# Whole-row attention units of a block-sparse attention + MLP kernel, spread over two chunks

## The chip, the cores and the metric

The kernel runs on one core of a Trainium2 chip. The metric is the device time of one execution in microseconds (us). Each core has TensorE (PE, with a separate row PEld for its weight loads), VectorE (DVE), ScalarE (ACT), GpSimd (POOL) and SyncE (SP, which here only issues transfers). Each engine takes its instructions in the order in which they were written for it and waits at semaphores for the others.

## The reference, cut to what matters

```python
batch, n_heads, seq, head_dim = (4, 8, 768, 64);  block = 32
scores = scale * q @ k.T                       # per batch and head
mask   = |blk_i - blk_j| <= 1  or  first/last block of queries or keys  or  3 sampled blocks per query block
attn   = softmax(where(mask, scores, -1e9));   a = attn @ v
x      = a as [3072 tokens, 512]
out    = relu(x @ w_in) ** 2 @ w_out           # d_ff = 2048
```

A query block in the middle of the sequence sees 8 key blocks. The first and the last query block of a batch (64 rows per head) see all 768 keys: these are the whole rows.

## The kernel before, in words

**Tiling.** The 3072 tokens are 24 tiles of 128, three tiles to a chunk, so 8 chunks, two to a batch. For a chunk the MLP runs over 16 slices `f` of d_ff: `hidden` (L894) makes 12 matmuls into a PSUM tile `ph`, ACT makes `r` (relu) and `gh` (its square, rounded), DVE `gf` (the square in full), POOL `gl = gf - gh`; two slices later `project` (L920) multiplies `gh` and `gl` with `wo` into three accumulators `po`. In that time `wi` and `wo` of a coming slice are split: a DVE cast (L847) for the high part and a POOL subtraction (L848) for the low part.

**Attention beside it.** While PE works on the MLP of chunk c, the attention of chunk c+1 is laid between its matmuls. There are two kinds of unit. A `Half` is one tile's sparse rows for four heads: scores `s` (PE), maxima `m` and difference `p` (DVE), 16 exps that also move 32x32 blocks to other partitions, `pm` (ACT, L481), a transpose `pT` (DVE, L487), values `pv` (PE), normalisation (DVE). A `Whole` is a batch's whole rows for one pair of heads, four to a batch (`pr` 0 to 3): scores `g` (PE, L624), maxima (DVE), two exps `pg` (ACT, L649), 16 copies of 32x192 blocks `pgm` that alternate between POOL and ACT (L660), a transpose `pTg` (DVE, L666), values `pvg` (PE, L694), normalisation (DVE).

**What sets the order.** The order is written out: the MLP is a generator, and each of its yields is one step, about 96 to a chunk and 6 to a slice `f`. A unit is a generator too; what it yields is the number of steps until its next part is issued. `LAG` holds these numbers. A half starts every 16 steps (`STEP`), six to a chunk. For a whole the parts stand at: scores 0, exps 4, copies from 8 (two in a step, so eight steps), transpose at 20, values at 39. What a step holds for an engine is put in that engine's queue at that place, and nothing passes it later.

**Where the wholes stood.** `units(c)` gave a batch's four wholes to its first chunk, 16 steps apart, each 6 steps (`G_AT`) behind a half. So all four wholes of batch 1 stand beside the MLP of chunk 0 (its end) and 1, those of batch 2 beside chunk 2 (its end) and 3, those of batch 3 beside chunk 4 (its end) and 5. Chunks 2 and 4 carry six halves and only the beginning of the next wholes.

**Buffers.** `pT` and `pTg` share two buffers. A half's `pT` is used 11 steps after its transpose (`v`), a whole's `pTg` 19 steps after (`w`). Split weights `wi`, `wo` and `pg`, `pgm` share seven buffers (tag `w`). There is one buffer for each half of the keys of a batch (`kn`), one for its values (`vn`, in two halves one after the other), and one for its whole-row queries (`QG`).

**Loads.** SP issues nearly all transfers in one queue. Keys of the next batch were asked for in the fifth tile of a batch (`NT - 2`), the whole-row queries and values in the sixth.

```python
LAG = {"s": 0, "e": 4, "v": 11, "x": 4, "t": 4, "c": 0, "v0": 13, "w0": 4, "w": 19, "n": -1}
```

Of the kernel before, what the change touches and what calls it, by code (L numbers as in the profile page):

```python
# [22 lines left out]
B, H, S, D = 4, 8, 768, 64  # L23
# [4 lines left out]
NT = S // P  # L28
NJ = P // BLK
NPAIR = H // 2  # L30
# [32 lines left out]
STEP = PIECES // (2 * UC)  # L63
EARLY = 23
LAST = 4
LAG = {"s": 0, "e": 4, "v": 11, "x": 4, "t": 4, "c": 0, "v0": 13, "w0": 4, "w": 19, "n": -1}

G_AT = 6

STEP_0 = 5  # L70
STEP_1, FIRST_1 = 12, 0
LAG_1 = {**LAG, "v": 10, "x": 3, "t": 6, "v0": 5, "n": 0}
LAG_0 = {"s": 2, "x": 2, "t": 3, "c": 2, "v0": 2, "n": 2, "r": 1, "l": 3, "l0": 8}
# [23 lines left out]
def tile_block_sparse_attention_moe(ctx: ExitStack, tc, kd, knd, qd, qgd, vd, vnd, samp, const, wcat, out):  # L97
# [9 lines left out]
    nc = tc.nc  # L107
# [63 lines left out]
    def load_whole(b, eng=nc.sync):  # L171

        eng.dma_start(QG.rearrange("p a b -> p (a b)"), qgd[b])

    def load_keys(b, u, eng=nc.sync):

        kn = rot.tile([P, NBLK, 2, BLK], F32, tag=f"kn{u}", name=f"kn{b}_{u}", bufs=1)
        eng.dma_start(kn.rearrange("p a b c -> p (a b c)"), knd[b, u])
        st["kn", b, u] = kn
# [18 lines left out]
    def load_static(k, u, eng=nc.sync):  # L198
        us = halves(k, u)
        if us is None:  # L200
            return
        n = 1 if k == 0 else NJ
        for i in range(us.start, us.stop):
            src = columns(vd[order[k][0], V_STATIC * BLK :], i)
            src = src.unsqueeze(1).broadcast_to([2 * BLK, n, HW // 2])
            eng.dma_start(values_of(k)[0][0 : 2 * BLK, i, 0:n], src)
# [29 lines left out]
    def load_vn(b, hf, eng=nc.sync, own=None):  # L236

        vn = (own or rot).tile([P, NT, HW // 2], F32, tag="vn", name=f"vn{b}_{hf}", bufs=1)
        eng.dma_start(vn.rearrange("p t c -> p (t c)"), vnd[b, hf])
        st["vn", b, hf] = vn  # L240
# [19 lines left out]
    def load_q(b, t, eng=nc.sync, own=None):  # L260
        q = (own or rot).tile([P, NJ, NPAIR, BLK], F32, tag="q", name=f"q{b}_{t}", bufs=1 if own else 2)
        n = NJ * NPAIR * BLK
        eng.dma_start(q.rearrange("p a b c -> p (a b c)"), qd[b, :, t * n : (t + 1) * n])
        st["q", b, t] = q

    def keys_of(b, t, own=None):

        k = order.index((b, t))
        st["kg", b, t] = own.tile([P, NJ, NK, NPAIR, BLK], F32, name=f"KG{k}") if own else KG[(k - (k >= UC)) % 2]
# [5 lines left out]
    def copy_keys(b, t):  # L275

        vals = sampled(t, 0, POOL)
        k, kg = order.index((b, t)), st["kg", b, t]
        for u in range(2):
            copy = nc.gpsimd.tensor_copy  # L280
            if t < UC:
                static_keys(b, t, u, copy)
            if 0 < k < UC:
                key_edges(k, u, copy)
            else:
                key_windows(k, u, copy)
            kn = st["kn", b, u]
            for j in groups(t):
                for r in range(NRAND):
                    copy(  # L290
                        kg[:, j, key_place(k, j, r), 2 * u : 2 * u + 2].unsqueeze(1),
                        kn[:, bass.ds(vals[NRAND * j + r], 1)],
                    )
                yield
# [24 lines left out]
    def load_kg(b, t):  # L319
        vals = sampled(t, 0, SP)  # L320
        keys_of(b, t)
        k, kg, js = order.index((b, t)), st["kg", b, t], groups(t)
        k4 = kd[b].rearrange("p (a c) -> p a c", a=NBLK)
        for j in js:
            for r in range(NRAND):
                nc.sync.dma_start(
                    kg[:, j, key_place(k, j, r)].rearrange("p b c -> p (b c)").unsqueeze(1),
                    k4[:, bass.ds(vals[NRAND * j + r], 1), :],
                )
        src = k4[:, NJ * t + js[0] - 1]  # L330
        src = bass.AP(src.tensor, src.offset, [[NBLK * P, P], [P, len(js)], [1, 3 * P]])
        nc.sync.dma_start(kg[:, js[0] : js[-1] + 1, NK - 3 :].rearrange("p j a b c -> p j (a b c)"), src)
# [7 lines left out]
    def load_window(k, u, eng=nc.sync):  # L340
        us = halves(k, u)
        if us is None:
            return
        b, t = order[k]
        VB = values_of(k)[1]
        js = sorted(groups(t))
        j, c, n = js[0], NJ * t + js[0], len(js)
        for i in range(us.start, us.stop):
            src = vd[b, (c - 1) * BLK : (c + 1 + n) * BLK, i * HW // 2 : (i + 1) * HW // 2]
            src = bass.AP(src.tensor, src.offset, [[HW, 3 * BLK], [BLK * HW, n], [1, HW // 2]])  # L350
            eng.dma_start(VB[BLK:P, i, j : j + n], src)

    def load_sampled(k, u, eng, on, which=range(NRAND)):
        us = halves(k, u)
        if us is None:
            return
        b, t = order[k]
        VA, VB = values_of(k)
        vals = sampled(t, 1, on)
        v4 = columns(vd[b], us).rearrange("(a p) u c -> p a u c", p=BLK)  # L360
        for j in sorted(groups(t)):
            for r in which:
                a = (place(k, j, 3) if r == 2 else 2 + r) * BLK
                dst = (VB if r == 2 else VA)[a : a + BLK, us, j]
                eng.dma_start(dst.unsqueeze(1), v4[:, bass.ds(vals[NRAND * j + r], 1)])
# [14 lines left out]
    class Half:  # L380
# [172 lines left out]
        def loads(self, step):  # L553

            k = order.index((self.b, self.t))
            eng = nc.gpsimd if self.b == 0 else nc.sync
            if step == 0 and self.t == NT - 2 and self.b + 1 < B:
                load_keys(self.b + 1, self.u, eng)
            if step == 0 and self.t == NT - 1 and self.b + 1 < B:
                if self.u == 0:  # L560
                    load_whole(self.b + 1, eng)
                    load_vn(self.b + 1, 0, eng)
            n = k + (UC if k < UC - 1 else UC - 1)
            if step == 0 and self.u == 1 and k != UC - 1 and n < len(order):
                load_q(*order[n])
                if n < 2 * UC:
                    keys_of(*order[n])
                    later.append(copy_keys(*order[n]))
                    next(later[-1])
                elif self.moved:  # L570
                    load_kg(*order[n])
            if step == 1 and self.u == 1 and 2 * UC <= n < len(order):
                load_kg(*order[n])
            n = UC if k == 0 else k + 1
            if step == 2 and k not in range(1, UC) and n < len(order):
                if self.t == NT - 1:
                    load_static(n, self.u)
                load_window(n, self.u)
                load_sampled(n, self.u, nc.sync, SP)

    class Whole:
# [71 lines left out]
        def move(self):  # L653

            self.pm = rot.tile([P, NJ, NT, BLK], F32, tag="w", name=f"pgm{self.name}", bufs=WBUFS)
            x = self.p.rearrange("p (k a s) -> p k a s", k=NT, a=NJ)
            for g in range(NJ):
                for a in range(NJ):
                    copy = nc.scalar.copy if a % 2 else nc.gpsimd.tensor_copy
                    copy(self.pm[a * BLK : (a + 1) * BLK, g], x[g * BLK : (g + 1) * BLK, :, a])  # L660
                    if a % 2:
                        yield 0

        def turn_blocks(self):
# [53 lines left out]
    def begins(c):  # L718

        return PIECES * c - min(c, 1) * LEAD * UC  # L720

    def units(c):

        halves = [Half(b, t, u) for b, t in order[c * UC : (c + 1) * UC] for u in range(2)]
        wholes = [] if c % 2 else [Whole(c // 2, pr) for pr in range(NPAIR)]
        if c == 0:
            return [(i * STEP_0, u) for i, u in enumerate(wholes + halves)]
        if c == 1:
            return [(i * STEP_1 + FIRST_1, u) for i, u in enumerate(halves)]
        at = begins(c - 1) - EARLY  # L730
        both = [(at + i * STEP, u) for i, u in enumerate(halves)]
        both += [(at + i * STEP + G_AT, u) for i, u in enumerate(wholes)]
        return sorted(both, key=lambda x: x[0])

    class Stream:
# [285 lines left out]
    first = copy_keys(0, 1)  # L1021
# [20 lines left out]
    for at, u in units(0):  # L1042
        work.add(at, 0, lambda u=u: u.run(side, LAG_0))
# [21 lines left out]
    for c in range(1, NCH):  # L1065
        for at, u in units(c):
            work.add(at, c, lambda u=u, lag=LAG_1 if c == 1 else LAG: u.run(bank, lag))
    now = 0
# [71 lines left out]
```

## Time and profile before

| what | value |
|---|---|
| time, median of 3 runs | 744.15 us (743.92 to 744.68) |
| the profiled execution, its own time | 745.86 us |
| its span, first to last instruction | 744.0 us |
| PE busy | 714.0 us, 96% of the span |
| PE weight loads busy | 569.7 us, 77% |
| DVE busy | 533.0 us, 72% |
| ACT busy | 500.5 us, 67% |
| POOL busy | 539.4 us, 73% |
| mean granted TensorE clock | 0.991 |

The profile is of one execution. A row of a group reads: line, engine, operation, output <- input, shapes, count, busy time and mean duration of one, then the idle time of the engine just before such instructions and who ended it. A row of the timeline reads: start, duration, engine, line, operation, count, and in brackets the idle time before it with the instruction that ended it. A row of waits reads: who waited for whom, total us, times, longest. Below, "stretch c" is the time from the first `ph` matmul of chunk c to that of chunk c+1; in it the MLP of chunk c and the attention of chunk c+1 run.

### The profile page before, as it was taken

How to read it: one execution, taken by the hardware profiler on the slowest of the kernel's cores; microseconds unless marked ns; L12 is line 12 of the kernel's file. 1: busy time of each engine (PE TensorE's matmuls, PEld its weight loads, DVE VectorE, ACT ScalarE, POOL GpSimd, SP SyncE). 2: the span in 40 equal slices, each digit the busy share in tenths (PEclk: the TensorE clock that was granted, in tenths of full speed). 3: DMA queues.
4: the chain of work that ended last, by engine and by line, in shares of the span. 5: the costliest groups of instructions: out<-in, count | busy, mean ns of one | idle time of the engine just before them, and what ended most of it. 6: DMA issues, size and time to landing. Idle time of an engine off the chain costs nothing.

```text
span 744.0 us, 21519 instructions
## 1 busy us (share of the span) xinstructions
PE 714.0 (96%) x7496; PEld 569.7 (77%) x7496; DVE 533.0 (72%) x1076; ACT 500.5 (67%) x1107; POOL 539.4 (73%) x681
## 2 busy tenths in 40 slices
PE   5869999999999999999999999999999999999997
PEld 2546666567878888877878888877778888888996
DVE  7885766968776877768877786768778686647552
ACT  5875677998875875579776777478866776623222
POOL 7986734249786587769877577877976586868985
PEclk9988999999999999999999999999999999999999
DMA  8785799755555547645455466455355452101001
GB/s 271 226 225 159 206 298 304 179 154 171 146 126 130 174 126 211 145 104 144 104 165 146 100 193 177 132 131 176 95 160 143 100 160 55 34 1 44 1 1 42
DMA packets 94479, 105.22 MB, mean 141 GB/s; under 512 B 13827, under 2 KB 82180, under 8 KB 94372
## 3 DMA queue, kind: packets, MB, share of 16 engines
q1 hardware_dynamic: 88420, 81.00, 41.1%
q0 software_dynamic: 5664, 22.45, 9.2%
q8 instruction: 60, 0.98, 0.6%
q14 instruction: 47, 0.39, 0.2%
q10 hardware_dynamic: 288, 0.39, 0.1%
HBM read 97.50 MB, written 6.29 MB: 140 GB/s over the span
## 4 chain that ended last, share of the span: by engine, by line
PE 72%; DVE 10%; ACT 8%; POOL 5%; issue 3%; DMA 1%; SPq 0%; POOLq 0%; ACTq 0%; DVEq 0%
PE ph L883 30%; PE po L936 26%; PE s L436 5%; PE pv L531 5%; PE po L926 3%; DVE m L448 2%; POOL gl L917 2%; PE pvg L694 2%; POOL pgm L660 1%; ACT craw L803 1%; ACT p L495 1%; POOL wo L848 1%; PE g L624 1%; DVE p L456 1%; DVE pT L487 1%
## 5 line engine op out<-in xcount | busy, mean ns | idle before, releaser
L883 PE MATMUL ph<-xh,wi 128*128 128x384 f32 x960 | 276.1, 348 | 0.6 <-POOL wi L848 0.4
L481 ACT ACTIVATE pm<-p 32x256 f32<-32x256 f32 x528 | 219.3, 415 | 15.4 <-DVE p L456 8.2
L848 POOL TENSOR_TENSOR wi<-W,wi 128x512 fp32r<-128x512 f32 x120 | 163.7, 1364 | 71.8 <-DVE wi L847 36.9
L936 PE MATMUL po<-wo,gh 128*128 128x512 f32 x672 | 211.7, 396 | 0.0
L883 PEld LDWEIGHTS ph<-xh,wi 128*128 128x128 f32 x960 | 173.9, 188 | 23.0 <-issue 10.0
L904 ACT ACTIVATE r<-ph 128x384 f32<-128x384 f32 x128 | 63.0, 492 | 168.2 <-PE ph L883 167.6
L848 POOL TENSOR_TENSOR wo<-WO,wo 128x512 fp32r<-128x512 f32 x112 | 144.9, 1293 | 34.6 <-DVE wo L847 32.9
L917 POOL TENSOR_TENSOR gl<-gf,gh 128x384 fp32r<-128x384 f32 x112 | 119.1, 1063 | 64.1 <-DVE gf L915 54.5
L883 PE MATMUL ph<-xl,wi 128*128 128x384 f32 x480 | 162.4, 338 | 0.0
L936 PEld LDWEIGHTS po<-wo,gh 128*128 128x128 f32 x672 | 123.0, 188 | 27.1 <-issue 7.5
L936 PE MATMUL po<-wo,gl 128*128 128x512 f32 x336 | 134.6, 401 | 5.1 <-POOL gl L917 4.9
L915 DVE SCALAR_TENSOR_TENSOR gf<-ph,r 128x384 f32<-128x384 f32 x112 | 62.0, 553 | 105.7 <-ACT r L904 97.6
L883 PEld LDWEIGHTS ph<-xl,wi 128*128 128x128 f32 x480 | 90.3, 188 | 7.6 <-issue 3.3
L847 DVE CAST wo<-WO 128x512 fp32r<-128x512 f32 x112 | 85.1, 760 | 0.0
L936 PEld LDWEIGHTS po<-wo,gl 128*128 128x128 f32 x336 | 63.0, 187 | 24.6 <-POOL gl L917 11.5
L910 ACT ACTIVATE gh<-r 128x384 fp32r<-128x384 f32 x112 | 59.0, 526 | 10.4 <-ACT r L904 0.4
L448 DVE TENSOR_REDUCE m<-s 128x2 f32<-128x512 f32 (+1 forms) x96 | 61.1, 676 | 3.0 <-PE s L436 3.0
L847 DVE CAST wi<-W 128x512 fp32r<-128x512 f32 x105 | 60.4, 576 | 0.0
L531 PEld LDWEIGHTS pv<-V,pT 128*32 128x32 f32 x2816 | 43.5, 111 | 20.6 <-issue 10.6
L531 PE MATMUL pv<-V,pT 128*32 128x65 f32 x2816 | 52.2, 224 | 5.1 <-DVE xn L548 1.9
L436 PE MATMUL s<-KG,q 64*32 64x256 f32 x1408 | 55.2, 391 | 0.8 <-issue 0.6
L456 DVE TENSOR_TENSOR p<-s,m 128x512 f32<-128x512 f32 (+1 forms) x72 | 45.9, 677 | 0.0
(92 smaller groups left out, 768.1 us busy)
## 6 DMA issues: line engine op xcount, KB each, us to landing
craw<-in_w_dram POOLq DMA_DIRECT2D x32, 512.0 KB, 5.9
V<-in_v_dram SPq DMA_DIRECT2D x462, 32.5 KB, 2.1
KG<-in_k_dram SPq DMA_DIRECT2D x198, 64.0 KB, 1.9
V<-in_v_dram SPq DMA_DIRECT2D x28, 390.0 KB, 5.5
KG<-in_k_dram SPq DMA_DIRECT2D x12, 768.0 KB, 5.9
q<-in_q_dram SPq DMA_DIRECT2D x24, 256.0 KB, 2.8
out_dram<-ot SPq DMA_DIRECT2D x22, 256.0 KB, 5.8
V<-in_v_dram SPq DMA_DIRECT2D x16, 292.5 KB, 6.3
```

What stands on the lines that cost most here:

```text
L436: nc.tensor.matmul(self.sb[e][g * BLK : (g + 1) * BLK, i * NSLOT : (i + 1) * NSLOT], q[r, j, pr, :], kg[r, j, :, pr, :], start=True, stop= ...
L448: nc.vector.tensor_reduce(m[at, e], self.sb[e][at].rearrange("p (i c) -> p i c", i=2), axis=AX, op=ALU.max)
L481: nc.scalar.activation(p[a * BLK : (a + 1) * BLK, g], x[g * BLK : (g + 1) * BLK, :, a], AF.Exp, scale=SCALE)
L531: nc.tensor.matmul(po[h * BLK : (h + 1) * BLK, g * VW : (g + 1) * VW], self.pT[:, g, 2 * e + i, c], v[:, self.u, j, h * VW : (h + 1) * VW] ...
L847: nc.vector.tensor_copy(w[:, 0], src)
L848: nc.gpsimd.tensor_tensor(w[:, 1], src, w[:, 0], op=ALU.subtract)
L883: nc.tensor.matmul(ph[c, f][:, :TOK], wi[:, w, cc], x[:, cc], start=(cc == 0 and i == 0), stop=(cc == NCC - 1 and i == 2),)
L904: nc.scalar.activation(r, acc[:, :TOK], AF.Relu)
L910: nc.scalar.activation(gh, r, AF.Square)
L915: nc.vector.scalar_tensor_tensor(gf, acc[:, :TOK], 0.0, r, op0=ALU.max, op1=ALU.mult)
L917: nc.gpsimd.tensor_tensor(gl, gf, gh, op=ALU.subtract)
L936: nc.tensor.matmul(acc[c][u], g[:, at], w[:, k], start=(f == 0 and i == 0), stop=(f == NF - 1 and i == 2))
```

## The change

Three things change.

1. A table `WHOLES` places the wholes. Batches 0 and 1 keep their places. Batches 2 and 3 have `pr` 0 and 1 in the chunk before (at 32 and 64 of its steps) and `pr` 2 and 3 in the batch's first chunk (at 16 and 48): 32 steps apart within a chunk, and 48 from `pr` 1 to `pr` 2. `pr` 2 now stands where `pr` 1 stood, `pr` 3 where it was.
2. For every whole of batches 1 to 3, the 16 block copies take 12 steps (first POOL and ACT one each, then POOL alone, then ACT alone, four times). They begin two steps earlier (`t` 4 to 2), the transpose comes one step later (at 21), the values at 39 as before.
3. The keys of the next batch, its whole-row queries and the first half of its values are asked for in a batch's fourth tile (`NT - 3`) instead of the fifth and sixth (batch 0 keeps its places).

```diff
-LAG = {"s": 0, "e": 4, "v": 11, "x": 4, "t": 4, "c": 0, "v0": 13, "w0": 4, "w": 19, "n": -1}
+LAG = {"s": 0, "e": 4, "v": 11, "x": 4, "t": 2, "c": 0, "v0": 13, "w0": 3, "w": 18, "n": -1}
+WHOLES = {
+    0: {pr: 0 for pr in range(4)},
+    1: {},
+    2: {pr: 16 * pr for pr in range(4)},
+    3: {0: 32, 1: 64},
+    4: {2: 16, 3: 48},
+}
@@ def loads(self, step):
-            if step == 0 and self.t == NT - 2 and self.b + 1 < B:
-                load_keys(self.b + 1, self.u, eng)
-            if step == 0 and self.t == NT - 1 and self.b + 1 < B:
...
+            elif step == 0 and self.t == NT - 3 and self.b + 1 < B:
+                load_keys(self.b + 1, self.u)
                 if self.u == 0:
-                    load_whole(self.b + 1, eng)
-                    load_vn(self.b + 1, 0, eng)
+                    load_whole(self.b + 1)
+                else:
+                    load_vn(self.b + 1, 0)
@@ def move(self):
-                    if a % 2:
+                    if a > 0:
                         yield 0
@@ def units(c):
-        wholes = [] if c % 2 else [Whole(c // 2, pr) for pr in range(NPAIR)]
+        b, at = (c + 1) // 2, WHOLES[c if c < 3 else 4 - c % 2]
+        wholes = [Whole(b, pr) for pr in at if b < B]
...
-        both += [(at + i * STEP + G_AT, u) for i, u in enumerate(wholes)]
+        both += [(first + at[u.pr] + G_AT, u) for u in wholes]
```

What it does to the queues is seen at three places. In the names, `gl3_7` is `gl` of chunk 3, slice 7; `pgm2_3` belongs to the whole `pr` 3 of batch 2; the last number of a name only counts tiles. The lines of the new kernel lie 13 lower.

POOL in stretch 3, from `gl` of slice 6 to `gl` of slice 7, before and then now:

```order
514 L917 TENSOR_TENSOR gl3_6_6665<-gf3_6_6663,gh3_6_6661 128x384
515 L660 COPY pgm2_3_6549<-pg2_3_6497 32x192
516 L848 TENSOR_TENSOR wi3_8_6676<-W18_1370,wi3_8_6676 128x512
517 L660 COPY pgm2_3_6549<-pg2_3_6497 32x192 x3
518 L848 TENSOR_TENSOR wo3_7_6697<-WO7_1382,wo3_7_6697 128x512
519 L660 COPY pgm2_3_6549<-pg2_3_6497 32x192 x2
520 L917 TENSOR_TENSOR gl3_7_6728<-gf3_7_6726,gh3_7_6724 128x384
```

```order
522 L930 TENSOR_TENSOR gl3_6_6688<-gf3_6_6686,gh3_6_6684 128x384
523 L672 COPY pgm2_3_6536<-pg2_3_6522 32x192
524 L861 TENSOR_TENSOR wi3_8_6698<-W18_1370,wi3_8_6698 128x512
525 L672 COPY pgm2_3_6536<-pg2_3_6522 32x192 x2
526 L861 TENSOR_TENSOR wo3_7_6717<-WO7_1382,wo3_7_6717 128x512
527 L672 COPY pgm2_3_6536<-pg2_3_6522 32x192
528 L930 TENSOR_TENSOR gl3_7_6747<-gf3_7_6745,gh3_7_6743 128x384
```

Six copies stood between the two `gl`, and two of them between the split of `wo` and `gl3_7`; now there are four, and one. On ACT six copies stood between `r3_6` and `r3_7`, now four.

ACT at the beginning of stretch 3, up to `r` of slice 0, before and then now:

```order
356 L481 ACTIVATE pm2_0_1_5864<-p2_0_1_5834 32x256 x5
357 L649 ACTIVATE pg2_1_5929<-g2_1_0_5873,mb2_1_5902 128x384
358 L649 ACTIVATE pg2_1_5929<-g2_1_1_5874,mb2_1_5902 128x384
359 L481 ACTIVATE pm2_0_1_5864<-p2_0_1_5834 32x256 x2
360 L947 COPY ot2_2_5943<-po2_2_4674 128x512
361 L481 ACTIVATE pm2_0_1_5864<-p2_0_1_5834 32x256 x2
362 L660 COPY pgm2_1_5964<-pg2_1_5929 32x192
363 L904 ACTIVATE r3_0_5971<-ph3_0_5953 128x384
```

```order
388 L488 ACTIVATE pm2_0_1_5951<-p2_0_1_5929 32x256 x5
389 L661 ACTIVATE pg2_2_6012<-g2_2_0_5958,mb2_2_5987 128x384
390 L661 ACTIVATE pg2_2_6012<-g2_2_1_5959,mb2_2_5987 128x384
391 L488 ACTIVATE pm2_0_1_5951<-p2_0_1_5929 32x256 x2
392 L672 COPY pgm2_2_6024<-pg2_2_6012 32x192
393 L960 COPY ot2_2_6029<-po2_2_4679 128x512
394 L488 ACTIVATE pm2_0_1_5951<-p2_0_1_5929 32x256 x2
395 L672 COPY pgm2_2_6024<-pg2_2_6012 32x192
396 L917 ACTIVATE r3_0_6056<-ph3_0_6039 128x384
```

The exps at this place are those of `pr` 2 and no longer of `pr` 1, and since the copies begin two steps earlier, two of them stand ahead of `r3_0` where there was one.

POOL in stretch 2, from `gl` of slice 8 to `gl` of slice 9, before and then now:

```order
455 L917 TENSOR_TENSOR gl2_8_5210<-gf2_8_5208,gh2_8_5206 128x384
456 L338 COPY KG1_85<-kn2_0_4631 128x4x2x64
457 L848 TENSOR_TENSOR wi2_10_5214<-W110_1372,wi2_10_5214 128x512
458 L848 TENSOR_TENSOR wo2_9_5357<-WO9_1384,wo2_9_5357 128x512
459 L917 TENSOR_TENSOR gl2_9_5385<-gf2_9_5383,gh2_9_5381 128x384
```

```order
462 L930 TENSOR_TENSOR gl2_8_5263<-gf2_8_5261,gh2_8_5259 128x384
463 L345 COPY KG1_85<-kn2_0_4156 128x4x2x64
464 L672 COPY pgm2_1_5267<-pg2_1_5245 32x192
465 L861 TENSOR_TENSOR wi2_10_5270<-W110_1372,wi2_10_5270 128x512
466 L672 COPY pgm2_1_5267<-pg2_1_5245 32x192 x2
467 L861 TENSOR_TENSOR wo2_9_5438<-WO9_1384,wo2_9_5438 128x512
468 L672 COPY pgm2_1_5267<-pg2_1_5245 32x192
469 L930 TENSOR_TENSOR gl2_9_5468<-gf2_9_5466,gh2_9_5464 128x384
```

Four copies of `pr` 1 of batch 2 are new between these two `gl`, and four more between `gl2_9` and `gl2_10`.

More of the change, by code (lines that the diff above doesn't have):

```diff
@@ L555, in loads @@
             k = order.index((self.b, self.t))
-            eng = nc.gpsimd if self.b == 0 else nc.sync
-            if step == 0 and self.t == NT - 2 and self.b + 1 < B:
-                load_keys(self.b + 1, self.u, eng)
-            if step == 0 and self.t == NT - 1 and self.b + 1 < B:
+            if step == 0 and self.b == 0:
+                if self.t == NT - 2:
+                    load_keys(1, self.u, nc.gpsimd)
+                if self.t == NT - 1 and self.u == 0:
+                    load_whole(1, nc.gpsimd)
+                    load_vn(1, 0, nc.gpsimd)
+            elif step == 0 and self.t == NT - 3 and self.b + 1 < B:
+                load_keys(self.b + 1, self.u)
                 if self.u == 0:
-                    load_whole(self.b + 1, eng)
-                    load_vn(self.b + 1, 0, eng)
+                    load_whole(self.b + 1)
+                else:
+                    load_vn(self.b + 1, 0)
             n = k + (UC if k < UC - 1 else UC - 1)
@@ L729, in units @@
             return [(i * STEP_1 + FIRST_1, u) for i, u in enumerate(halves)]
-        at = begins(c - 1) - EARLY
-        both = [(at + i * STEP, u) for i, u in enumerate(halves)]
-        both += [(at + i * STEP + G_AT, u) for i, u in enumerate(wholes)]
+        first = begins(c - 1) - EARLY
+        both = [(first + i * STEP, u) for i, u in enumerate(halves)]
+        both += [(first + at[u.pr] + G_AT, u) for u in wholes]
         return sorted(both, key=lambda x: x[0])
```

## The prediction

> **What bounds the kernel now.** I read the page first, then a table of the stretches, then the waits inside them, then the timeline around each wait of PE.
>
> ```profile
> PE 714.0 (96%) x7496; PEld 569.7 (77%) x7496; DVE 533.0 (72%) x1076; ACT 500.5 (67%) x1107; POOL 539.4 (73%) x681
> PE 72%; DVE 10%; ACT 8%; POOL 5%; issue 3%; DMA 1%; SPq 0%; POOLq 0%; ACTq 0%; DVEq 0%
> ```
>
> PE is the bound, and nothing in the change takes a matmul away. So it can gain only where PE stands still for another engine. The table of windows (length, busy time of PE, PEld, DVE, ACT, POOL) shows where:
>
> ```profile
> 161.30:250.30 89.00, 87.64 (x994) 72.22 (x993) 69.21 (x153) 67.71 (x159) 66.19 (x72) 1.00 0.52 139
> 250.30:332.60 82.30, 82.30 (x865) 68.53 (x865) 60.02 (x113) 56.92 (x131) 62.72 (x58) 1.00 0.59 157
> 332.60:422.20 89.60, 87.74 (x994) 71.29 (x992) 69.71 (x154) 68.00 (x159) 66.42 (x72) 1.00 0.50 132
> 422.20:504.50 82.30, 82.30 (x866) 68.54 (x864) 60.78 (x112) 56.89 (x131) 62.72 (x58) 1.00 0.57 156
> 504.50:594.00 89.50, 87.66 (x993) 71.31 (x992) 69.60 (x154) 67.91 (x159) 66.42 (x72) 1.00 0.50 134
> ```
>
> These are stretches 1 to 5. The odd ones, with the wholes, are 7.2 us longer, with about 9 us more of DVE and 11 us more of ACT. Part of it is matmul work that no placing removes:
>
> ```profile
> L694 PE MATMUL pvg<-vn,pTg 128*64 128x65 f32 x384 | 15.9, 233 | 2.6 <-ACT pTg L681 2.0 <-DVE pTg L683 0.7
> ```
>
> 15.9 us over 16 wholes is 1.0 us each, 4.0 for four. (The scores `g` are two wholes' in each stretch, since `pr` 0 and 1 are scored at the end of the stretch before.) That leaves 7.2 - 4.0 = 3.2 us. The waits of stretch 3 (first two rows), of stretch 4 and of stretch 1 say what it is:
>
> ```profile
> PEld po L936 <- POOL gl L917: 3.8, 5, 1.6
> DVE pTg L666 <- PE pvg L694: 5.9, 3, 2.8
> PEld po L936 <- POOL gl L917: 0.3, 1, 0.3
> PEld po L936 <- POOL gl L917: 2.2, 2, 1.6
> ```
>
> Weight loads wait 3.8 us for `gl` in stretch 3, 0.3 in stretch 4, 2.2 in stretch 1; in stretch 5 the first two rows stand again with the same numbers. 3.8 - 0.3 = 3.5 is nearly the 3.2 left. So what can be gained lies in POOL's `gl` coming late.
>
> **How much each late `gl` costs PE.** Here are four places, two rows each, the first pair undisturbed:
>
> ```profile
> 328.29 0.64 PE L936 MATMUL po<-wo,gh 128*128 128x512 f32 x2
> 328.76 0.40 PE L936 MATMUL po<-wo,gl 128*128 128x512 f32 x1
> 377.90 0.63 PE L936 MATMUL po<-wo,gh 128*128 128x512 f32 x2
> 379.67 0.50 PE L936 MATMUL po<-wo,gl 128*128 128x512 f32 x1 [1.15 <-POOL gl L917]
> 350.23 0.63 PE L936 MATMUL po<-wo,gh 128*128 128x512 f32 x2
> 350.96 0.50 PE L936 MATMUL po<-wo,gl 128*128 128x512 f32 x1
> 338.94 0.72 PE L936 MATMUL po<-wo,gh 128*128 128x512 f32 x2
> 340.07 0.50 PE L936 MATMUL po<-wo,gl 128*128 128x512 f32 x1 [0.41 <-POOL gl L917]
> ```
>
> Undisturbed, `gl` follows `gh` by 0.47 us. At slice 7 it follows by 1.77, a loss of 1.30; at slice 2 by 0.73, a loss of 0.26; at slice 0 by 1.13, a loss of 0.66.
>
> **The copies in 12 steps (stretches 1, 3, 5).** Why is `gl3_7` late?
>
> ```profile
> 369.72 0.49 ACT L904 ACTIVATE r<-ph 128x384 f32<-128x384 f32 x1 [1.99 <-PE ph L883]
> 375.62 0.49 ACT L904 ACTIVATE r<-ph 128x384 f32<-128x384 f32 x1
> 376.21 0.56 DVE L915 SCALAR_TENSOR_TENSOR gf<-ph,r 128x384 f32<-128x384 f32 x1 [1.20 <-POOL pgm L660]
> 376.27 1.29 POOL L848 TENSOR_TENSOR wo<-WO,wo 128x512 fp32r<-128x512 f32 x1
> 377.63 0.91 POOL L660 COPY pgm<-pg 32x192 f32<-32x192 f32 x2
> 378.62 0.99 POOL L917 TENSOR_TENSOR gl<-gf,gh 128x384 fp32r<-128x384 f32 x1
> 381.13 0.98 DVE L666 STREAM_TRANSPOSE pTg<-pgm 128x768 f32<-128x768 f32 x1 [2.80 <-PE pvg L694]
> 389.05 2.10 PE ph L883 x12
> 391.16 2.08 PE po L936 x9
> L660 POOL COPY pgm<-pg 32x192 f32<-32x192 f32 x96 | 36.7, 382 | 4.4
> L660 ACT COPY pgm<-pg 32x192 f32<-32x192 f32 x96 | 33.6, 350 | 1.3
> ```
>
> Two delays add up. ACT comes to `r` of slice 7 at 375.62, 5.9 us after `r` of slice 6, while PE needs 2.10 + 2.08 = 4.2 us for a slice (the two rows of the chain): `r` is about 1.7 late. Then `gf` ends at 376.77, but POOL goes through `wo` and two copies until 378.6: another 1.8 late. Of 3.5 the slack of two slices swallows 2.2, and 1.3 is left for PE. The change leaves four of six copies on each engine between the slices: ACT gains 2 x 0.35 = 0.7, and POOL has one copy less ahead of `gl`, 0.38 to 0.46; the earlier `gf` alone doesn't help, but the split of `wo` also comes earlier by up to the other missing copy, 0.38. Together 0.8 (POOL alone) to 1.5 (both delays), so the 1.3 falls to between 0 and 0.5; I take 0, the end at which both delays shrink, since in stretches 3 and 5 the whole before this one (`pr` 2) has besides finished its copies well ahead and no longer holds POOL and ACT up. **-1.3** in each of stretches 1, 3 and 5.
>
> **The DVE waits (stretches 3 and 5).** Before, a whole's transpose stands 16 steps behind the last whole's, at its step 20, whose buffer is free at 39: 3 steps early, with the other buffer held by a half. Hence 5.9 us in which DVE holds its whole queue, casts and `gf` with it. With wholes 32 steps apart the transpose is due at 32 + 21 = 53 against 39: no wait. PE pays for this only at slice 2, 0.26, since most of the wait is taken while DVE has nothing urgent behind it (after 381.13 no `gl` comes late until the end of the stretch). **-0.3** each. In stretch 1 the wait shrinks by one step of three and I count nothing.
>
> **The beginning of the stretches.** Here `r` of slice 0 is late already, and the change puts one copy more ahead of it:
>
> ```profile
> 337.41 0.35 ACT L660 COPY pgm<-pg 32x192 f32<-32x192 f32 x1
> 337.78 0.49 ACT L904 ACTIVATE r<-ph 128x384 f32<-128x384 f32 x1
> ```
>
> The 0.66 at slice 0 becomes 1.0: **+0.35** in stretches 3 and 5. `pTg` of `pr` 0 no longer stands here on DVE (0.98), but `r`, not DVE, is last, so it returns nothing. In stretch 1, where no `gl` is late here, I count 0 to 0.35, and take **+0.1**.
>
> **Two wholes each in stretches 2 and 4.** They bring 2 x 8 copies of POOL, 6 us, beside the 62.72 of 82.30 us. The tightest place is slices 8 to 10, where also a copy of keys stands. In stretch 4 before:
>
> ```profile
> 468.10 1.30 POOL L848 TENSOR_TENSOR wo<-WO,wo 128x512 fp32r<-128x512 f32 x1 [0.37 <-DVE wo L847]
> 471.04 1.04 POOL L917 TENSOR_TENSOR gl<-gf,gh 128x384 fp32r<-128x384 f32 x1 [1.65 <-DVE gf L915]
> 474.77 1.20 POOL L917 TENSOR_TENSOR gl<-gf,gh 128x384 fp32r<-128x384 f32 x1
> 477.77 0.40 PE L936 MATMUL po<-wo,gl 128*128 128x512 f32 x1
> ```
>
> Ahead of `gl4_9` POOL is idle for 0.37 + 1.65 = 2.0, room for the four new copies (1.5). `gl4_10` ends at 475.97 and is used at 477.77; four more copies make it 477.5, which just holds. From below 0, from above the whole 1.5 in each; I take **+0.1** each, by the 0.3 that is left.
>
> A rule of the Trainium skill speaks against this term, and this row bears on it (min, median, max in ns of one cast):
>
> ```profile
> L847 DVE CAST wo<-WO x112: 377/552/1521, 164.4 to 732.3; 128x512 fp32r<-128x512 f32 x112
> ```
>
> The same cast takes from 0.38 to 1.5 us, so something holds it up. The Trainium skill, "SBUF — State Buffer", section "SBUF: two separate sides", says that GpSimd and some VectorE operations share one pair of ports, and that whichever comes second is blocked until the first has ended; the row agrees in kind. By this rule POOL's four copies would also wait for the two casts between `gl4_9` and `gl4_10`.
>
> In rows: if the copies also wait for the two casts there, at their median of 0.55, that makes 1.1 us, `gl4_10` ends at 478.6, and PE loses 0.8 in each of two stretches. The sum below would be 1.4 us smaller. I take the idle time as it stands, since the POOL durations used here already hold what such collisions cost before.
>
> **The earlier loads.**
>
> ```profile
> SPq L351 <- PE pv L531: 50.0, 17, 7.8
> kn<-in_kn_dram SPq DMA_DIRECT2D x4, 768.0 KB, 4.4
> ```
>
> `kn`, `QG` and `vn` pass V windows, sampled blocks and a `q` in SP's queue. SP itself waits 50 us in all for values to be done, up to 7.8 at a time, and that covers the issue. Without that cover a V window would land later by one 4.4 us transfer, against 32 steps from one tile's values to the next (a third of a stretch, 27 us). The whole needs its keys 38 steps after they are asked for. Both cost 0, as do the lookup of the table and the shorter `LAG` entries, whose sum is unchanged (values at 39).
>
> **The sum.** -1.3 x 3 - 0.3 x 2 + 0.35 x 2 + 0.1 + 0.1 x 2 = -3.5 us. The profiled execution took 745.86 (span 744.0), and the runs have a median of 744.15; the difference is taken off the median, as the waits lie inside the span. 744.15 - 3.5 = 740.65, forecast **740.6 us**.
>
> **The rivals.**
>
> *More goes than I count* (734.5 to 737.5). All `gl` waits of the odd stretches vanish, 2.2 + 3.8 + 3.8 = 9.8, or most of them: 734.4 at the best. For it: wholes 32 apart leave a pause on all three engines. Against it: the wait at slice 0 stays by its place in the queue, and the one at a stretch's end (0.3) stands in stretch 4 too, without wholes. I give 0.12 to at least 6.6.
>
> *Nothing is gained* (743 to 745). The delay of `r` at slice 7 comes from the half's exps and the last whole's copies together, and the last whole keeps its place. If the thinner copies only move the delay, -0.3 x 2 is eaten by +0.35 x 2 and 744.3 is left. For it: two of three engines are as full on average as before, and copies that leave one slice land in the next. Against it: the copies of `pr` 2 no longer stand in the slices just before. Chance 0.15.
>
> *Slower: the stall goes with the wholes.* Each of the four wholes that moved to stretches 2 and 4 takes the 1.3 us of a late `gl` with it, because a key copy and eight POOL copies now fall where the slack of `gl4_10` is 1.8 us. 4 x 1.3 = 5.2 more, and with one of the three slice-7 stalls still gone and the beginnings dearer by 0.8, 744.15 + 5.2 - 1.3 + 0.8 = 748.9. It decides from the point where two slices hold over 1.8 + 2.0 us of new POOL work; I count 3.0. Against it also: in stretches 2 and 4 ACT is 11 us freer. Chance 0.07.
>
> *The ports.* POOL and DVE hold each other up, as worked out above from the cast's row: -3.5 + 1.4 = -2.1, 742.0. Chance 0.10.
>
> That the change doesn't do what it says I exclude: the queues show the wholes moved and the copies thinned.
>
> **How the numbers follow.** The forecast, with its own range from 738.0 to 742.0 (the slice-7 stalls fall to between 0 and 0.5 each, slice 0 costs 0 to 0.7, stretches 2 and 4 cost 0 to 0.5), has 0.56; the rivals 0.12, 0.15, 0.07 and 0.10. A measurement of this kernel tells about 0.2% (1.5 us) from no change, so faster means under 742.66. Faster: 0.56 + 0.12 + 0.10 = 0.78. Same: 0.15. Slower: 0.07. For 8 in 10 the range takes the forecast, the ports, the nearer part of the larger gain and the nearer part of no gain: 737.3 to 743.5.
>
> **What would show it.** Stretches 1, 3 and 5 get shorter, 3 and 5 also by two `pvg`, 2.0 us, and one whole's scores, which moved to 2 and 4 and lengthen them as much. The waits for `pvg` ahead of `pTg` vanish in stretches 3 and 5 and remain, shorter, in 1; the 1.58 us wait at slice 7 vanishes in all three; the wait at slice 0 of stretches 3 and 5 grows from 0.83 to about 1.2 us of idle weight loads; stretches 2 and 4 show no wait for `gl` beyond their 0.3. I am wrong if a wait at slice 7 stays above 0.8, if stretches 2 and 4 show a wait of over 0.5 at slices 9 or 10, or if PE comes to wait for something else (a `wi` split, V, or keys).

## The result: slower by half a percent

The changed kernel takes 748.53 us (median of 6 runs, 748.26 to 749.98) against 744.51 us (6 runs). The ratio is 1.0051, with a 95% interval of 1.0040 to 1.0063. Timed once more beside the experiments it was 748.57 against 745.52, ratio 1.0038 (1.0025 to 1.0051). The forecast was 740.6, faster. The profiled execution took 748.47 us, its span is 746.4.

### The profile after

The table of windows of the changed kernel, stretches 1 to 5, with the columns as before (length, then busy PE, PEld, DVE, ACT, POOL):

```profile
161.10:249.50 88.40, 87.86 (x994) 72.27 (x993) 70.98 (x152) 67.97 (x159) 66.47 (x72) 1.00 0.54 148
249.50:334.90 85.40, 85.40 (x922) 70.07 (x921) 63.01 (x133) 60.85 (x141) 64.87 (x66) 1.00 0.56 151
334.90:423.10 88.20, 85.05 (x937) 69.64 (x936) 64.69 (x133) 64.06 (x149) 63.82 (x64) 1.00 0.53 135
423.10:508.40 85.30, 85.30 (x921) 70.08 (x920) 62.98 (x133) 60.73 (x141) 64.91 (x66) 1.00 0.55 151
508.40:596.50 88.10, 85.19 (x938) 69.69 (x937) 65.67 (x134) 64.17 (x149) 63.42 (x64) 1.00 0.48 126
```

Stretch 1 is 0.6 us shorter. Stretches 2 and 4 are 3 us longer, by the matmul work of the wholes that came to them, and PE is busy in all of it. Stretches 3 and 5 lost 2.7 and 2.5 us of busy PE time and are only 1.4 us shorter. So each pair of stretches takes 1.6 to 1.7 us more than before (171.9 and 171.8 then, 173.6 and 173.4 now), though its work is the same. The loss lies in stretches 3 and 5 alone.

The waits of the changed kernel in stretch 3 (four rows), stretch 2 (one), stretch 1 (two). In its lines the wholes stand 12 lower than before, not 13: L636, L672, L678 and L706 are `g`, `pgm`, `pTg` and `pvg`.

```profile
PEld po L949 <- POOL gl L930: 4.7, 5, 1.3
DVE pTg L678 <- POOL pgm L672: 4.1, 2, 2.4
PEld po L949 <- ACT gh L923: 0.7, 1, 0.7
PEld po L949 <- POOL wo L861: 0.4, 1, 0.4
PEld po L949 <- POOL gl L930: 0.3, 1, 0.3
DVE pTg L678 <- PE pvg L706: 4.4, 2, 2.4
PEld po L949 <- POOL gl L930: 1.4, 2, 0.8
```

The wait of DVE for `pvg` is gone in stretch 3, as forecast; where it stood, DVE now waits for POOL's copies. PE waits 5.8 us for `gl`, `gh` and `wo` together, where it waited 4.1 before (3.8 for `gl`, 0.3 for `gh`). The timeline of PE in stretch 3 has the four places in pairs, first `gh` and then `gl` of slices 0, 1, 2 and 7 (0.47 us apart when undisturbed):

```profile
341.69 0.73 PE L949 MATMUL po<-wo,gh 128*128 128x512 f32 x2 [0.42 <-ACT gh L923]
342.91 0.50 PE L949 MATMUL po<-wo,gl 128*128 128x512 f32 x1 [0.49 <-POOL gl L930]
346.74 0.63 PE L949 MATMUL po<-wo,gh 128*128 128x512 f32 x2
347.74 0.50 PE L949 MATMUL po<-wo,gl 128*128 128x512 f32 x1 [0.37 <-POOL gl L930]
351.54 0.94 PE L949 MATMUL po<-wo,gh 128*128 128x512 f32 x2
353.48 0.50 PE L949 MATMUL po<-wo,gl 128*128 128x512 f32 x1 [0.99 <-POOL gl L930]
380.41 0.63 PE L949 MATMUL po<-wo,gh 128*128 128x512 f32 x2
381.66 0.50 PE L949 MATMUL po<-wo,gl 128*128 128x512 f32 x1 [0.62 <-POOL gl L930]
```

Slice 7 loses 1.25 - 0.47 = 0.8 us (1.3 before). Slices 0 to 2 lose 0.75, 0.53 and 1.47, and slice 0 another 0.42 at `gh`: 3.2 us together, against 0.66 + 0.26 = 0.9 before. By slice that is +0.5, +0.5 and +1.2, in all +2.2 at the start, and -0.5 at slice 7. It makes +1.7, which is what the pair of stretches lost.

What else changed at the start is seen when ACT and PE are laid side by side. The timeline of ACT, from `r` of the last slice to `r` of slice 0, first of the kernel before (its `r` of slice 0 at 337.78 stands in the prediction), then of the changed one:

```profile
328.49 0.49 ACT L904 ACTIVATE r<-ph 128x384 f32<-128x384 f32 x1 [0.43 <-PE ph L883]
```

```profile
330.74 0.49 ACT L917 ACTIVATE r<-ph 128x384 f32<-128x384 f32 x1 [0.80 <-PE ph L896]
340.53 0.49 ACT L917 ACTIVATE r<-ph 128x384 f32<-128x384 f32 x1
```

ACT needs 9.3 us for this before and 9.8 after, where PE has some 6.4 us of its own work (330.7 to 337.1 in its timeline after): it enters slice 1 behind in both kernels. The half microsecond more is mostly the copy that I counted (0.35), and it explains slice 0. But then the kernel before has two pieces of PE work in slices 1 and 3, in its timeline:

```profile
341.89 0.88 PE L624 MATMUL g<-kn,QG 64*64 64x384 f32 x8
348.56 0.92 PE L694 MATMUL pvg<-vn,pTg 128*64 128x65 f32 x24
```

The changed kernel has neither there: `pr` 2 is scored where `pr` 1 was, and the values of `pr` 0 are done in stretch 2. The exps and copies of the whole that remains at the start are as many as before, and so are the casts and splits of the MLP. (The second whole's maxima and exps, `pr` 2's own, stood in slices 1 to 3 before and are gone from there: 1.05 us of ACT. That brought `gl` no sooner.) The timeline of POOL has `gl` of slice 2, before and after:

```profile
349.89 1.02 POOL L917 TENSOR_TENSOR gl<-gf,gh 128x384 fp32r<-128x384 f32 x1
```

```profile
352.42 1.00 POOL L930 TENSOR_TENSOR gl<-gf,gh 128x384 fp32r<-128x384 f32 x1
```

Counted from the start of the stretch (332.6 and 334.9) it ends at 18.3 us before and 18.5 after, and `gl` of slice 1 at 12.7 and 12.8. Neither row has idle time in brackets: POOL was busy up to it in both. PE, with 2 us less to do, comes to `gh` of slice 2 at 16.6 us and no longer at 17.6, although it has waited more at slices 0 and 1, and there it waits again.

### The profile page after: what moved, and what is told of

Read it like the earlier page. It is cut to its first block, busy times and chain, and to the rows that moved or that the text cites. A ratio compares the mean times of both kernels' runs of the same rounds, so it can differ in the third digit from the quotient of the medians.

```text
span 746.4 us, 21520 instructions
## 1 busy us (share of the span) xinstructions
PE 715.0 (96%) x7496; PEld 570.1 (76%) x7496; DVE 531.7 (71%) x1076; ACT 500.7 (67%) x1107; POOL 538.0 (72%) x681
## 4 chain that ended last, share of the span: by engine, by line
PE 72%; DVE 12%; ACT 8%; POOL 4%; issue 2%; DMA 1%; SPq 1%; POOLq 0%; ACTq 0%; DVEq 0%
PE ph L896 30%; PE po L949 26%; PE s L443 5%; PE pv L538 5%; PE po L939 3%; DVE m L455 3%; PE pvg L706 2%; PE g L636 1%; POOL gl L930 1%; DVE p L463 1%; ACT r L917 1%; DVE gf L928 1%; DVE pT L494 1%; POOL wo L861 1%; ACT craw L816 1%
## 5 line engine op out<-in xcount | busy, mean ns | idle before, releaser
L896 PEld LDWEIGHTS ph<-xh,wi 128*128 128x128 f32 x960 | 173.6, 188 | 24.2 <-issue 11.6
L860 DVE CAST wo<-WO 128x512 fp32r<-128x512 f32 x112 | 81.8, 730 | 0.1
L860 DVE CAST wi<-W 128x512 fp32r<-128x512 f32 x105 | 62.6, 596 | 0.0
```

Source lines behind the costliest of these rows:

```text
L860: nc.vector.tensor_copy(w[:, 0], src)
L896: nc.tensor.matmul(ph[c, f][:, :TOK], wi[:, w, cc], x[:, cc], start=(cc == 0 and i == 0), stop=(cc == NCC - 1 and i == 2),)
```

## The experiments

Three theories of the loss: **A**, the stall is lost cover, that is, PE work moved away from slices where the other engines set the pace while a whole's exps and copies stayed; **B**, the copies that begin two steps earlier hold up `r` and `gl`; **C**, the earlier loads stand ahead of others in SP's queue and make PE wait.

### The table of places, with the old copies

```diff
 # against the changed kernel
-LAG = {..., "t": 2, ..., "w0": 3, "w": 18, ...}
+LAG = {..., "t": 4, ..., "w0": 4, "w": 19, ...}
-                    if a > 0:
+                    if a % 2:
```

> The change's table of places and its early loads, with the old copies (two in a step, eight steps, from step 8). Theory A (cover): the stall at the start of stretches 3 and 5 comes from the matmul work that moved away from slices 1 to 3 (scores of one whole, values of another, 1 us each) while exps and copies of a whole stay there. It remains here, with one copy less ahead of r of slice 0; the late gl of slice 7 stays too (1.3 us each). So slower than before by 3 to 4 us, about 748. Theory B (early copies): the stall comes from the copies beginning two steps earlier. Then it is gone here, and 743 to 744 is left.

750.42 us, ratio to the kernel before 1.0071 (1.0057 to 1.0084). Its window and main wait in stretch 3:

```profile
335.40:424.10 88.70, 85.16 (x938) 69.73 (x937) 65.25 (x133) 64.04 (x149) 63.38 (x64) 1.00 0.49 129
PEld po L949 <- POOL gl L930: 5.3, 5, 1.6
```

The early loads are still in this run. The old copies make it worse, not better, so B falls: moving the wholes costs 0.7% without the new copies. (That the loads have no part in it is shown two runs further on.)

### The copies alone

```diff
 # against the kernel before
-LAG = {..., "t": 4, ..., "w0": 4, "w": 19, ...}
+LAG = {..., "t": 2, ..., "w0": 3, "w": 18, ...}
-                    if a % 2:
+                    if a > 0:
```

> The change's copies in 12 steps from step 6, with the old places of the wholes and the old loads. Theory A: all the matmul work is still at the start of the stretches, so slice 0 costs 0.35 to 0.7 us more in stretches 3 and 5, and slice 7 gets 0.6 better in 1, 3 and 5: 743 to 744.5. Theory B: the start of stretches 3 and 5 loses the 2.2 us more that the whole change showed there: about 747 to 748.

744.99 us, ratio 0.9997 (0.9988 to 1.0006): no difference. Stretches 1 and 3:

```profile
159.60:248.00 88.40, 87.86 (x995) 72.17 (x994) 71.02 (x152) 67.99 (x159) 66.45 (x72) 1.00 0.50 139
330.20:419.60 89.40, 87.72 (x993) 71.35 (x993) 71.89 (x155) 68.46 (x160) 66.80 (x72) 1.00 0.50 133
```

Stretch 1 gains the same 0.6 us as in the whole change, stretch 3 gains 0.2: slice 7 gives back 0.6 there, and slice 0, behind the earlier copies, takes 0.4. So in the whole change the copies in sum are no part of the loss.

### The loads alone

```diff
 # against the kernel before: loads() of the changed kernel, nothing else
+            elif step == 0 and self.t == NT - 3 and self.b + 1 < B:
+                load_keys(self.b + 1, self.u)
...
```

> The old kernel with only the keys, whole-row queries and values of batches 2 and 3 asked for a tile or two earlier. Theories A and B: within 0.5 us of before. Theory C (loads): the earlier loads sit in SP's queue ahead of V and key loads and make PE wait: 746 to 748, with waits for DMA in stretches 2 and 4.

745.67 us, ratio 1.0004 (0.9995 to 1.0013): no difference, so C falls.

### The wholes away from the start of the stretches

```diff
 # against the changed kernel
-    4: {2: 16, 3: 48},
+    4: {2: 32, 3: 64},
```

> The whole change, but in a batch's first chunk the wholes stand at 32 and 64 of its steps instead of 16 and 48, so that no whole's exps or copies fall on the start of stretches 3 and 5. Theory A and B both: the waits for gl at slices 0 to 2 vanish there, and the time falls below before, to 738 to 741. Theory C: no better than the change, 747 to 749.

740.0 us, ratio 0.9927 (0.9913 to 0.9940): faster than both kernels. Stretches 2 and 3, and all the wait for `gl` that is left in stretch 3:

```profile
249.70:334.30 84.60, 84.45 (x914) 69.88 (x912) 63.09 (x133) 60.83 (x141) 64.98 (x66) 1.00 0.54 149
334.30:419.00 84.70, 84.48 (x945) 70.10 (x944) 63.02 (x133) 64.09 (x149) 63.71 (x64) 1.00 0.53 138
PEld po L949 <- POOL gl L930: 0.6, 1, 0.6
```

The pair takes 169.3 us, 2.6 less than before and 4.3 less than the change, with the same four wholes. Nothing but the place of `pr` 2 and `pr` 3 differs. This holds under A and under B alike; what tells them apart are the table with the old copies and the next run. POOL's `gl` of slice 2 is now ready 14.6 us into the stretch (348.87 - 334.3) instead of 18.5, because a whole's exps and copies no longer stand ahead of it:

```profile
347.83 1.04 POOL L930 TENSOR_TENSOR gl<-gf,gh 128x384 fp32r<-128x384 f32 x1 [0.87 <-DVE gf L928]
```

### The cover put back

```diff
 # against the changed kernel
+    class Fill(Whole):
+        def run(self, bank, lag):
+            self.scores()
+            yield 0
 ...
+        if c in (4, 6):
+            both += [(first + x, Fill(b, pr)) for x, pr in ((38, 2), (45, 3))]
```

This run adds work whose result nobody reads. The changed kernel was timed again beside it:

> The changed kernel itself, as the measure for the run with added matmuls: about 748.5 by all theories.

> The changed kernel with matmul work put back at the start of stretches 3 and 5: the scores of two wholes are computed a second time into banks that nobody reads, one at the step where the old kernel had pr 2's scores (slice 1), one where it had pr 0's values (slice 3). That is 2 x 1.0 us of added PE work in each of two stretches, 4 us in all. Theory A (the stall at the start is lost cover: ACT and POOL set the pace there, not PE): PE would have waited in that time, so the kernel gets only 0 to 1.2 us slower than the change. Rival (a fixed stall, whatever PE does): 4 us slower than the change, about 752.5.

748.72 us with the added matmuls, 748.57 without; ratios to the kernel before 1.0041 (1.0028 to 1.0054) and 1.0038. The four added scores take 0.88 us each, 3.5 us of PE work in all (the expectation put 4), and cost nothing that can be told. In the run with added matmuls, stretch 3, its PE timeline at slices 0 to 2 (`gh` and `gl` in pairs, the added scores behind the first two), and `gl` of slice 2 on POOL:

```profile
335.40:423.70 88.30, 86.52 (x953) 70.02 (x953) 65.46 (x134) 64.14 (x149) 63.67 (x64) 1.00 0.53 134
342.28 0.73 PE L957 MATMUL po<-wo,gh 128*128 128x512 f32 x2 [0.46 <-ACT gh L931]
343.51 0.50 PE L957 MATMUL po<-wo,gl 128*128 128x512 f32 x1 [0.50 <-POOL gl L938]
345.32 0.88 PE L636 MATMUL g<-kn,QG 64*64 64x384 f32 x8
348.32 0.63 PE L957 MATMUL po<-wo,gh 128*128 128x512 f32 x2
348.79 0.40 PE L957 MATMUL po<-wo,gl 128*128 128x512 f32 x1
351.19 0.88 PE L636 MATMUL g<-kn,QG 64*64 64x384 f32 x8
353.52 0.63 PE L957 MATMUL po<-wo,gh 128*128 128x512 f32 x2
354.07 0.50 PE L957 MATMUL po<-wo,gl 128*128 128x512 f32 x1
353.01 1.01 POOL L938 TENSOR_TENSOR gl<-gf,gh 128x384 fp32r<-128x384 f32 x1
```

The stretch has 1.5 us more of busy PE and is 0.1 us longer. At slice 1 the wait for `gl` is gone (0.47 apart), because PE now gets there later, and at slice 2 the loss falls from 1.47 to 0.08 (0.55 apart). So 1.9 us of waiting went for 1.8 us of added work. Slice 0, which has no added work ahead of it, loses as much as in the change. And `gl` of slice 2 ends 18.6 us into the stretch (354.02 - 335.4), where it ended at 18.3 and 18.5: whether PE has this work or not, `gl` comes at nearly the same time. A stands: in slices 1 and 2 of these stretches PE is not the bound.

### The old copies with the wholes away from the start

```diff
 # against the kernel with the wholes at 32 and 64: the old LAG and copies, as in the first run
```

> Wholes away from the start (32 and 64 of the steps in both chunks), but with the old copies, two in a step. If the thinner copies are worth something by themselves, slice 7 of stretch 1 gets its 1.3 us back and gl of slice 10 in stretches 2 to 5, which has 0.6 us to spare with the thin copies, comes late by up to 0.5: 741.5 to 743. If only the place counts: 740 to 740.7.

740.5 us, ratio 0.9935 (0.9922 to 0.9948). Stretches 1 and 3:

```profile
161.30:250.30 89.00, 87.67 (x994) 72.23 (x993) 69.16 (x153) 67.79 (x159) 66.07 (x72) 1.00 0.55 148
334.90:419.60 84.70, 84.49 (x945) 70.08 (x944) 62.77 (x133) 64.09 (x149) 63.60 (x64) 1.00 0.55 139
```

Stretch 3 is as short as with the thin copies: that they might matter at slice 10 is not borne out. The 12 steps are worth 0.4 us in stretch 1 and nothing elsewhere once the wholes stand well.

### Batch 1 too

```diff
 # against the kernel with the wholes at 32 and 64
-    2: {pr: 16 * pr for pr in range(4)},
+    2: {0: 0, 1: 32, 2: 48, 3: 64},
```

> As the kernel with the wholes at 32 and 64, and batch 1's wholes at 0, 32, 48 and 64 of their chunk instead of 0, 16, 32 and 48, so that stretch 1 begins without a whole's exps too. Theory A: stretch 1 has no wait for gl at its start (0.6 us to spare), so nothing is to be had there: within 1 us of 740.0.

738.79 us, ratio 0.9913 (0.9900 to 0.9926), the fastest here. It is 1.2 us under the 740.0 of the kernel with the wholes at 32 and 64, a little more than expected, but the intervals of the two ratios overlap. Stretch 1, and its wait for `gl`:

```profile
159.90:248.50 88.60, 88.40 (x1003) 72.36 (x1001) 70.03 (x154) 68.84 (x161) 66.01 (x72) 1.00 0.56 149
PEld po L949 <- POOL gl L930: 0.6, 1, 0.6
```

There was nothing to be had at the start of stretch 1, as expected; the wait that vanished is the one of slice 7, since the copies of `pr` 2 and `pr` 3 now fall elsewhere. The stretch is as long with one whole's scores more in it (they left the stretch before). From the beginning of stretch 1 on the two kernels take 577.1 and 577.3 us (737.0 - 159.9, 738.4 - 161.1), so what was gained, if anything, was gained ahead of it.

## Why the prediction was wrong, point by point

**What bounds the kernel:** PE, and a gain only from the late `gl`. That held, and the time followed these waits. But the reading stopped at where PE waits. It did not ask which engine sets the pace in the slices around a wait, nor what PE work there hides how far the others are behind.

**The step that failed** is "The beginning of the stretches", +0.35 in stretches 3 and 5. It took the place with its PE work unchanged, added one copy, and priced it at slice 0 alone. There it was nearly right (+0.5). Slices 1 and 2, which it put at nothing, lost 1.7 more, so the step should have been +2.2. The prediction itself says that values and scores move from the odd to the even stretches, and counted that as neutral, work leaving one stretch and lengthening another. It was not: 2 us of it left the start, where ACT and POOL were behind and PE would have waited anyway. There they bought nearly nothing (1.7 of the 2 us came back as waiting), while in stretches 2 and 4 they were paid in full. The run with matmuls put back shows this, and so does the one with the wholes at 32 and 64.

**The copies in 12 steps** (-1.3 in stretches 1, 3 and 5): the mechanism was right, the size not. The loss at slice 7 falls from 1.3 to 0.5, 0.8 and 0.6 in stretches 1, 3 and 5, where 0 was forecast and 0.5 was its upper end; in stretch 3 the weight loads still wait 1.05 us there, over the 0.8 named as a sign of being wrong. The prediction took 0 because the whole before (`pr` 2) has finished early. With the copies alone, where it has not, slice 7 loses 0.7 in stretch 3, no more than in the change, so that bought nothing. What keeps the rest of the delay was not tested. The copies alone gained nothing that can be told.

**The DVE waits** (-0.3): the wait for `pvg` vanished in stretches 3 and 5 as worked out. At slice 2, where it was to pay, the new stall of 1.47 stands in its place.

**Two wholes each in stretches 2 and 4** (+0.1 each): held. No wait for `gl` beyond the 0.3 that was there. The prediction counted 2 x 8 copies more for POOL; its instructions rise by 8 only (58 to 66), since those of one whole already stood at the end of these stretches. The cast's price by the ports, 0.8 a stretch, did not appear either.

**The earlier loads** (0): held.

**The rivals.** Slower came with a chance of 0.07, by a stall that goes with the wholes to stretches 2 and 4. The sign was right and the mechanism wrong: there they ran free, and the loss stayed where they had been. That its 748.9 lies so near the measured 748.5 is luck. That `pr` 2 takes the place of `pr` 1 at the start, so that spreading leaves the densest place as dense as it was, stood in the order of the instructions; with it belonged the rival "the dense place stays and loses its cover".

In the spans the change is +2.4 us, from the beginning of stretch 1 on +2.6 (746.4 - 161.1 against 744.0 - 161.3). Of the 6.1 us from the forecast -3.5 to this +2.6, some 4.4 lie in slices 0 to 2 of stretches 3 and 5 (counting 5 like 3) and some 1.8 in slice 7. By the medians the change is +3.1 and +4.0. The two profiled executions differ by 2.6 in their own times too (748.47 against 745.86): the one of the kernel before is a long one, 1.4 us over its median of 744.51, and beside the experiments that median was 745.5. So the half to one and a half microsecond by which the medians go beyond 2.6 lies in no stretch that the profiles show; why executions of one kernel differ by as much stays open.

## What to carry to other kernels

Before work is moved, ask at each slice it leaves which engine sets the pace there. Where another engine is behind, as here in slices 1 and 2, taking work from the bound engine gave nearly nothing back, and where it landed it was paid in full. When units are spread out, look at the densest place first, and whether one of them still stands there afterwards; placing `pr` 2 and `pr` 3 another 16 steps later took this change from 0.4 to 0.5% slower than before to 0.7% faster. A wait row tells where the bound engine stands still, not how much work may be taken away in front of it without the wait growing by as much.

## What was not expected of the hardware

The added matmuls, 3.5 us put ahead of places where PE waits, lengthened the kernel by 0.15 us, less than its runs spread (747.4 to 749.4). And the time to the beginning of stretch 1 is not fixed: in the profiled executions it is 161.3 us before and 160.8 with the loads alone, which has the same instructions up to there, and 161.1 and 161.7 in two executions of the changed kernel. Spans of single executions of this kernel are therefore compared from that point on.
